# Nine transposes in a row over two PSUM banks with one copy per row half, and some loads in another order

## The chip, the core and the metric

The kernel runs on one core of a Trainium2 chip. The metric is the device time of one execution in microseconds (us), the median of several runs. The kernel before was run three times: 373.53, 374.88 and 376.76 us, so its median is 374.88 us.

Names of the engines: PE is TensorE (matmuls, and transposes as a matmul against an identity), DVE is VectorE, ACT is ScalarE, POOL is GpSimd, SP is the engine that only issues DMAs here. POOL issues DMAs too, and each costs it time. PSUM has 8 banks; PE writes its results there and DVE or ACT copy them out.

## What is computed

Causal attention with a running bias, then a gated feed-forward block over its output, all in one kernel:

```python
scores = q @ k.T / sqrt(64)                    # 8 batches x 8 heads, 576 positions, 64 wide
cum    = cumsum(max(s, 0))
scores = where(causal, -1e9, scores + min(-(cum_i - cum_j), 0))
x      = softmax(scores) @ v                   # -> 4608 tokens x 512
g      = x @ w_gate                            # 512 x 1536
out    = (g * sigmoid(g) * (x @ w_val)) @ w_out    # 1536 x 512
```

Inputs and output are float32; the kernel works in bfloat16 with float32 sums.

## The kernel before, in words

**Units of work.** The 64 heads are taken four at a time: 16 half-batches of four heads. The token rows of the feed-forward block come in 9 tiles of 512 tokens. For one tile 12 gate products and 12 value products of 4 matmuls each are made (lines 643 to 689), then the product with the output weights (line 700, or line 749 with a seven-product scheme in later tiles). The attention of batch b+1 runs between the matmuls of tile b: `ffn_items` yields after each small piece of tile work, and `pump` lets a matching amount of attention work out. All engines run their instructions in the order in which the Python code issues them, so this order is written by hand.

**k and q of a half-batch.** `load_one` brings a [128, 2, 9, 64] float32 tile of k or q; a cast makes it bfloat16 (`cast_one`, `cast_half`). Partition x holds 9 neighbouring positions j, so a half-batch needs 9 transposes of [128, 128] for k and 9 for q, one per j. Rows 0 to 63 of a transposed block belong to one pair of heads, rows 64 to 127 to the other. The blocks lie in PSUM in two groups, j = 0..4 in one bank and j = 5..8 in another (`JG`, line 45). Each group is copied out twice, once for each row half: `pe_out` (line 319) copies a [64, 640] or a [64, 512] block into `KQ`, re-ordering (j, x) into (x, j). So k alone needs four copies, two of 640 and two of 512 elements per partition. From half-batch 5 on, k and q go through DRAM and a DMA transpose instead (`scratch`, `transposes`, `split`).

**PSUM banks.** `take` (line 125) hands out the bank that was given back longest ago, `give` marks it free; this is done while the program is built. At run time an instruction that writes a bank waits for the last reader of that bank.

**The opening (lines 949 to 1033).** Half-batch 0 is prepared by row halves (`row_half`, `row_out`), in the fixed banks `EARLY` = 0, 1 for k and 2, 3 for q. Half-batch 1 is prepared by `half_batch`, which takes four banks; its second row halves are copied after `scores(3)` (lines 996 to 998). POOL casts, issues the loads of v, k, q and of the weights; SP issues others. For half-batch 2 `prep_one` (line 540) is called with i = 0 (k, first group), 1 and 3 (q, both groups) at lines 1026 to 1032, and with i = 2 (k, second group) at item 2 of the first feed-forward tile. `prep_one` copies the first row half at once and puts the copy of the second half on the list `seconds`: that of k is popped at line 1027, those of q one per feed-forward item. k goes to ACT, q to DVE. In between stand the first three gate products, begun by `begin` with the contraction parts that are there (lines 1021 to 1030).

**Hooks.** `at_item(n, ...)` runs a step when tile 0 has done n items (an item is a gate or a value product, 1.0 each, while there are 24 of them). Before: the casts of half-batch 3 at items 9 and 10 and the two halves of the output weights, `w_load("o", 0)` and `w_load("o", 1)`, at items 11 and 13. The casts of batch 1's v (`cast_v`, line 173) are issued on POOL in that same stretch. `load_qk(5)` was issued on SP at line 1016.

Of the kernel before, what the change touches and what calls it, by code (L numbers as in the profile page):

```python
# [13 lines left out]
BF16 = mybir.dt.bfloat16  # L14
# [5 lines left out]
def kernel(  # L20
# [11 lines left out]
    nc = tc.nc  # L32
    PSUM = bass.MemoryType.PSUM

    B, H, S, D = q.shape
# [7 lines left out]
    NR = HB // 2  # L43
    J = 9
    JG = ((0, 5), (5, 9))
# [18 lines left out]
    def pt_col(tj, bi):  # L64
# [26 lines left out]
    KQ = [  # L91
        [const.tile([128, 2, NR * S + 64], BF16, name=f"kq{e}{i}") for e in range(2)]
        for i in range(2)
    ]
    VT = [const.tile([128, NCH, H, D + 1], BF16, name=f"vt{i}") for i in range(2)]
    ident = const.tile([128, 128], BF16)
# [17 lines left out]
    with tc.manual_schedule():  # L114
        loaded = {}
        SRC = {"q": (q, 0), "k": (k, 1)}

        psb = ctx.enter_context(tc.tile_pool(name="psb", bufs=1, space=PSUM))
        banks = psb.tile([128, 8, 512], FP32, name="banks")
        bank = {i: banks[:, i, :] for i in range(8)}  # L120
        released = {i: i - 8 for i in bank}
        clock = [0]
        OPEN = 1 << 40

        def take():
            b = min(bank, key=lambda x: released[x])
            assert released[b] < OPEN
            released[b] = OPEN
            return b

        def give(b):
            clock[0] += 1
            released[b] = clock[0]

        def view(b, w):
            return bank[b][:, 0:w]

        def view16(b, w):
            return bank[b][:, 0 : w // 2].bitcast(BF16)

        def load_one(hb, name, rs=(0, NR), eng=nc.sync):
            b, g = divmod(hb, 2)
            if rs[0] == 0:
                loaded[name, hb] = raw.tile([128, NR, J, D], FP32, tag="raw" + name, name="raw" + name)
            eng.dma_start(
                loaded[name, hb][:, rs[0] : rs[1], :, :].rearrange("x r j d -> x r (j d)"),
                SRC[name][0][b, g * HB + 2 * rs[0] : g * HB + 2 * rs[1], :, :].rearrange(
                    "(r e) (p j) d -> (e p) r (j d)", e=2, j=J
                ),
            )  # L150

        def load_qk(hb):
            load_one(hb, "k")
            load_one(hb, "q")
# [12 lines left out]
        def cast_v(b, c, eng):  # L167
            n = 128 if c < 4 else TAIL
            dst, src_t = VT[b % 2][0:n, c, :, 0:D], loaded["v", b][0:n, c, :, :]
            if eng is nc.scalar:  # L170
                nc.scalar.copy(dst, src_t)
            else:
                eng.tensor_copy(dst, src_t)  # L173
# [79 lines left out]
        def cast_one(hb, name, eng):  # L253
            cts[name, hb] = cp.tile([128, J, NR, D], BF16, tag="c" + name, bufs=2, name="c" + name)
            dst = cts[name, hb].rearrange("x j r d -> x r j d")
            src_t = loaded[name, hb]
            if eng is nc.scalar:
                nc.scalar.copy(dst, src_t)
            else:
                eng.tensor_copy(dst, src_t)  # L260
# [32 lines left out]
        tps = {}  # L293

        def pe_transpose(hb, name, g):
            j0, j1 = JG[g]
            bs = take()
            ps = view16(bs, (j1 - j0) * 128).rearrange("p (j x) -> p j x", x=128)
            ct = cts[name, hb]
            for j in range(j0, j1):  # L300
                nc.tensor.transpose(  # L301
                    ps[:, j - j0, :], ct[:, j].rearrange("x r d -> x (r d)"), ident
                )
            tps[name, g] = [ps, bs, 2]

        def pe_transpose_half(hb, name, g, r):
            j0, j1 = JG[g]
            if r == 0:
                bs = EARLY[name][g]
                ps = view16(bs, (j1 - j0) * 128).rearrange("p (j x) -> p j x", x=128)  # L310
                tps[name, g] = [ps, bs, 2]
            ps = tps[name, g][0]
            ct = cts[name, hb]
            for j in range(j0, j1):
                nc.tensor.transpose(
                    ps[64 * r : 64 * r + 64, j - j0, :], ct[:, j, r, :], ident
                )

        def pe_out(hb, name, g, r, eng):
            j0, j1 = JG[g]  # L320
            kq = SRC[name][1]
            dst = KQ[hb % 2][r][64 * r : 64 * r + 64, kq, 0 : NR * S].rearrange(
                "a (x j) -> a x j", j=J
            )[:, :, j0:j1]
            tp = tps[name, g]
            srcp = tp[0][64 * r : 64 * r + 64].rearrange("a j x -> a x j")
            if eng is nc.scalar:
                nc.scalar.copy(dst, srcp)
            else:
                eng.tensor_copy(dst, srcp)  # L330
            tp[2] -= 1
            if tp[2] == 0:
                give(tp[1])

        def w_load(kind, j, h=None):
            dst = {"g": WG, "v": WV, "o": WO}[kind][j]
            if kind == "o":
                src_ap = moe_w_out[j * WKO * 128 : (j + 1) * WKO * 128, :].rearrange(
                    "(c p) n -> p c n", p=128
                )  # L340
            else:
                w = moe_w_gate if kind == "g" else moe_w_val
                lo, hi = (0, WCH) if h is None else (h * WCH // 2, (h + 1) * WCH // 2)
                src_ap = w[:, j * WCH + lo : j * WCH + hi].rearrange("(c p) n -> p c n", p=128)
                dst = dst[:, :, lo:hi]
            nc.gpsimd.dma_start(dst, src_ap)
# [191 lines left out]
        seconds = []  # L538

        def prep_one(hb, i, eng=None):  # L540
            g, nm = divmod(i, 2)
            nm = ("k", "q")[nm]
            pe_transpose(hb, nm, g)
            if eng is None:
                eng = nc.scalar if nm == "k" else nc.vector
            pe_out(hb, nm, g, 0, eng)
            seconds.append(lambda: pe_out(hb, nm, g, 1, eng))

        PREP_AT = {
            2: {(1, 3): 0, (2, 1): 2, (2, 3): 1, (3, 1): 3},  # L550
# [339 lines left out]
            else:  # L890
                yield from down_seven(tt, hps, sus)

        EARLY = {"k": (0, 1), "q": (2, 3)}
        PICK = (6, 4)
        for i in bank:
            released[i] = OPEN
# [1 line left out]
        def keep_warm(n, b):  # L898
            for _ in range(n):
                nc.tensor.matmul(view(b, 128), ident, ident, start=True, stop=True)  # L900

        def row_half(nm, r):
            for g in range(2):
                pe_transpose_half(0, nm, g, r)

        def row_out(nm, r, *engs):
            for g in range(2):
                pe_out(0, nm, g, r, engs[g])

        def pick(side):  # L910
            b = PICK[side]
# [20 lines left out]
            give(b)  # L932
            give(b + 1)

        def half_batch(nm):
            for g in range(2):
                pe_transpose(1, nm, g)
                pe_out(1, nm, g, 0, nc.vector)

        def scores(h):  # L940
            for ci in range(4):
                score_piece(h, ci)
# [8 lines left out]
        cast_half(0, "q", 0, nc.scalar)  # L951
        aug(0, SP4, range(1, HB))
        aug(1, SP4)
        row_half("k", 0)
        row_out("k", 0, nc.scalar, nc.scalar)
        cast_half(0, "k", 1, nc.gpsimd)
        cast_half(0, "q", 1, nc.gpsimd)
        load_v(0, range(5), nc.gpsimd)
        row_half("q", 0)
        pick(1)  # L960
        pick(0)
        pe_out(0, "q", 0, 0, nc.scalar)
        pe_out(0, "q", 1, 0, nc.vector)
        picked_row(1)
        picked_row(0)
        row_half("k", 1)
        score_piece(0, 0)
        score_piece(0, 1)
        row_half("q", 1)
        row_out("k", 1, nc.vector, nc.vector)  # L970
        cast_one(1, "k", nc.vector)
        row_out("q", 1, nc.vector, nc.vector)
        score_piece(0, 2)
        score_piece(0, 3)
        cast_one(1, "q", nc.gpsimd)
# [6 lines left out]
        load_one(2, "q", eng=nc.gpsimd)  # L982
        w_load("v", 0, 0)
        w_load("v", 0, 1)
        for nm in ("g", "v"):
            w_load(nm, 1, 0)
        load_one(3, "k", eng=nc.gpsimd)
        scores(1)
        half_batch("k")
        score_piece(2, 0)  # L990
        score_piece(2, 1)
        half_batch("q")
        score_piece(2, 2)
        score_piece(2, 3)
        scores(3)
        for nm in ("k", "q"):
            for g in range(2):
                pe_out(1, nm, g, 1, nc.vector)
        cast_v(0, 4, nc.vector)
        aug(2, SP4)  # L1000
        cast_one(2, "k", nc.gpsimd)
        cast_one(2, "q", nc.gpsimd)
        load_one(3, "q", eng=nc.gpsimd)
        for nm in ("g", "v"):
            w_load(nm, 1, 1)
        init_vt(1)
# [6 lines left out]
        aug(3, SP4)  # L1013
        load_v(1, range(5))
        load_qk(4)
        load_qk(5)
        x_pe(0, nc.vector)
        values(4, 5)
        x_pe(1, nc.scalar)
# [3 lines left out]
        begin("g", 1, range(2))  # L1023
        begin("g", 2, range(2))
        x_pe(3, nc.vector)
        prep_one(2, 0)
        while seconds:
            seconds.pop(0)()
        for ft in range(3):
            begin("g", ft, range(2, 3))  # L1030
        for i in (1, 3):
            prep_one(2, i)
        first_sbuf.close()
        PTP[0] = ctx.enter_context(tc.tile_pool(name="later", bufs=1))
        PTP["bufs"] = 5
# [15 lines left out]
        def at_item(n, f, *args):  # L1051
            hook[n].append(lambda: f(*args))

        at_item(2, prep_one, 2, 2)
        at_item(9, cast_one, 3, "k", nc.gpsimd)
        at_item(10, cast_one, 3, "q", nc.gpsimd)
        at_item(11, w_load, "o", 0)
        at_item(13, w_load, "o", 1)
        for tt in range(NTT):
            lo = H * (tt + 1) + LAGS[tt]  # L1060
            hi = min(H * (tt + 2) + LAGS[tt + 1], BH + 2)
# [4 lines left out]
            n = 0  # L1066
# [54 lines left out]
```

## Time and profile before

| what | before |
|---|---|
| median of 3 runs | 374.88 us (373.53 to 376.76) |
| the profiled execution's own time | 373.92 us |
| its span, first to last instruction | 372.0 us |
| granted TensorE clock, mean | 0.998 |
| busy: PE, DVE, ACT, POOL | 363.2, 291.1, 239.9, 212.4 us |
| PE idle between 0 and 20 us / 20 and 30 / 30 and 40 / 40 and 60 | 3.57 / 0.00 / 0.78 / 0.15 us |
| mean busy share of the DMA engines from 20 to 60 us, by tens | 1.17, 1.20, 1.23, 1.11 |

Times in a profile count from the start of the span. "L330" is line 330 of the kernel before. In a view of the chain, each row is a start, a length and the work that the next row waited for or followed; it is followed back from the end of the window. In a table of groups, a row gives line, engine and operation, the shapes, the count, the busy time in us, the mean length of one in ns, and the idle time of the engine ahead of it. In a table of stretches each engine has its busy time and, in brackets, its count, then come the granted clock, the DMA share and GB/s. PE's rows are pipelined: a 128-column transpose is shown with 219 ns, while five in a row start 55 ns apart.

### The profile page before, as it was taken

To read this page: it belongs to the slowest core of one execution; us is meant where nothing else is said; L and a number is where in the kernel's file an instruction comes from. 1 tells how busy PE (TensorE), PEld (TensorE's weight loads), DVE (VectorE), ACT (ScalarE), POOL (GpSimd) and SP (SyncE) were. 2 spreads that over 40 slices of the span, in tenths; PEclk is the share of its full clock that TensorE was granted. 3 is DMA by queue.
4 is the path that set the end of the run, shared out by engine and by line. 5 is a ranking of instruction groups with operands and counts; after the bars stand their busy time and mean duration, and the time that the engine had idled before them with its cause. 6 is when DMAs were issued, how large, how long until landed. Compare 5 with 4: busy or idle time off the path is not lost.

```text
span 372.0 us, 8786 instructions
## 1 busy us (share of the span) xinstructions
PE 363.2 (98%) x3288; PEld 230.3 (62%) x3288; DVE 291.1 (78%) x585; ACT 239.9 (65%) x470; POOL 212.4 (57%) x325
## 2 busy tenths in 40 slices
PE   7899999999999999999999999999999999999996
PEld 6684556655555557855685558655865585476465
DVE  8978776377985899589967897699868867975984
ACT  8877776778886967688757875786565523323321
POOL 8983556955266547594749464955675516315320
PEclk9999999999999999999999999999999999999999
DMA  7999999799879996996789484994142113002003
GB/s 238 220 254 259 215 272 257 239 299 227 252 172 307 199 268 181 162 285 217 214 179 263 160 185 157 265 210 114 40 121 62 35 30 118 0 3 86 28 0 113
DMA packets 97133, 64.21 MB, mean 173 GB/s; under 512 B 77228, under 2 KB 82724, under 8 KB 97092
## 3 DMA queue, kind: packets, MB, share of 16 engines
q1 hardware_dynamic: 84964, 41.46, 46.9%
q0 software_dynamic: 12128, 22.21, 22.7%
q8 instruction: 25, 0.41, 0.5%
q14 instruction: 16, 0.13, 0.1%
HBM read 37.90 MB, written 19.86 MB: 155 GB/s over the span
## 4 chain that ended last, share of the span: by engine, by line
PE 83%; DVE 10%; DMA 2%; ACT 2%; issue 2%; POOL 1%; DVEq 0%; ACTq 0%
PE banks L643 43%; PE banks L749 17%; PE banks L373 9%; PE banks L410 7%; PE banks L700 5%; DVE kq L330 3%; DMA pk<-ks 2%; DVE pp L666 2%; DVE ht L677 1%; DVE kq L288 1%; ACT th L664 1%; POOL vt L173 1%; ACT pt L383 1%; PE banks L459 1%; PE banks L301 0%
## 5 line engine op out<-in xcount | busy, mean ns | idle before, releaser
L383 ACT ACTIVATE pt<-banks 128x512 bf16<-128x512 f32 (+1 forms) x256 | 120.4, 511 | 29.8 <-PE banks L373 17.1
L643 PE MATMUL banks<-XT,wg 128*128 128x512 bf16 x432 | 111.4, 379 | 0.4 <-DVE pp L666 0.3
L643 PE MATMUL banks<-XT,wv 128*128 128x512 bf16 x432 | 110.9, 379 | 0.1
L664 ACT ACTIVATE th<-banks 128x512 bf16<-128x512 f32 x108 | 64.7, 599 | 56.3 <-PE banks L643 51.4
L666 DVE SCALAR_TENSOR_TENSOR pp<-th,banks 128x512 bf16<-128x512 bf16 x108 | 73.7, 682 | 18.3 <-ACT th L664 18.0
L677 DVE SCALAR_TENSOR_TENSOR ht<-pp,banks 128x512 bf16<-128x512 bf16 x108 | 74.1, 687 | 10.3
L373 PE MATMUL banks<-kq 128*128 128x128 bf16 (+4 forms) x576 | 76.4, 240 | 0.8 <-DVE kq L330 0.3
L686 POOL TENSOR_TENSOR ht<-ht 128x512 bf16<-128x512 bf16 x35 | 40.4, 1154 | 53.3 <-DVE su L684 53.2
L373 PEld LDWEIGHTS <-kq 128*128 128x128 bf16 x576 | 46.1, 98 | 30.7 <-issue 2.4
L643 PEld LDWEIGHTS <-wv 128*128 128x128 bf16 x432 | 38.4, 98 | 36.2 <-issue 0.2
L643 PEld LDWEIGHTS <-wg 128*128 128x128 bf16 x432 | 38.4, 98 | 34.1 <-issue 0.7
L410 PEld LDWEIGHTS <-pt 128*128 128x128 bf16 x960 | 41.8, 98 | 17.7 <-issue 0.7
L388 POOL TENSOR_SCALAR_AFFINE_SELECT pt<-pt 128x512 bf16<-128x512 bf16 x56 | 36.6, 653 | 25.9 <-ACT pt L383 21.7
L410 PE MATMUL banks<-vt,pt 128*128 128x65 bf16 x960 | 46.8, 194 | 0.5 <-DVE ot L427 0.4
L444 POOL DMA_DIRECT2D xs<-ot x24 | 21.7, 904 | 30.4 <-DVE ot L427 28.0
L749 PEld LDWEIGHTS <-ht 128*128 128x128 bf16 x336 | 31.2, 98 | 4.3
L427 DVE TENSOR_TENSOR ot<-banks,rc 128x320 bf16<-128x320 f32 x64 | 31.5, 492 | 2.2
L188 POOL DMA_DIRECT2D kq<-HL x48 | 29.2, 610 | 0.0
L700 PE MATMUL banks<-wo,ht 128*128 128x512 bf16 x96 | 25.8, 379 | 0.0
L749 PEld LDWEIGHTS <-su 128*128 128x128 bf16 x252 | 23.6, 98 | 3.3
L814 POOL TENSOR_TENSOR ysb<-ysb 128x512 f32<-128x512 f32 x12 | 15.2, 1269 | 15.3 <-DVE ysb L808 15.3
L749 PE MATMUL banks<-WS,ht 128*128 128x256 bf16 x168 | 22.9, 273 | 0.0
(101 smaller groups left out, 377.2 us busy)
## 6 DMA issues: line engine op xcount, KB each, us to landing
out_dram<-ysb POOLq DMA_DIRECT2D x32, 256.0 KB, 4.0
rawv<-in_v_dram SPq DMA_DIRECT2D x28, 256.0 KB
rawk<-in_k_dram SPq DMA_DIRECT2D x12, 576.0 KB
rawq<-in_q_dram SPq DMA_DIRECT2D x12, 576.0 KB
xs<-ot POOLq DMA_DIRECT2D x24, 160.0 KB, 3.7
ks<-ck SPq DMA_DIRECT2D x11, 288.0 KB
qs<-cq SPq DMA_DIRECT2D x11, 288.0 KB
rawk<-in_k_dram POOLq DMA_DIRECT2D x3, 576.0 KB, 6.0
```

What stands on the lines that cost most here:

```text
L373: nc.tensor.matmul(sc[:, o : o + w], T[:, 1, e * S + 128 * tj : e * S + 128 * (tj + 1)], T[:, 0, e * S + lo : e * S + hi], start=not maske ...
L383: nc.scalar.activation(pt[:, c0 : c0 + n], sc, AF.Exp, scale=0.125)
L388: nc.gpsimd.affine_select(pt[:, 1088:1600], pt[:, 1088:1600], pattern=[[0, 4], [1, 128]], compare_op=ALU.is_ge, fill=zreg, base=0, channel ...
L410: nc.tensor.matmul(av[:, bi * (D + 1) : (bi + 1) * (D + 1)], pt[:, c0 : c0 + 128], VT[b % 2][:, tj, h, :], start=(tj == 0), stop=(tj == bi),)
L427: nc.vector.tensor_mul(ot[:, :, e * D : (e + 1) * D], av3[:, :, 0:D], rc[:, :, None].to_broadcast([128, NCH, D]),)
L643: nc.tensor.matmul(view(bs, TT), w[:, c, f0 : f0 + 128], xt[:, c, :], start=(c == 0), stop=(c == 3),)
L664: nc.scalar.activation(th, pg, AF.Tanh, scale=0.5)
L666: nc.vector.scalar_tensor_tensor(pp, in0=th, scalar=1.0, in1=pg, op0=ALU.add, op1=ALU.mult)
L677: nc.vector.scalar_tensor_tensor(hp[:, 2 * k2 : 2 * k2 + 2, :].rearrange("p a n -> p (a n)"), in0=pp, scalar=0.5, in1=pv, op0=ALU.mult, op ...
L686: (nc.vector if ft == NFT - 1 else nc.gpsimd).tensor_sub(hp[:, 1:3, :], hp[:, 1:4:2, :], hp[:, 0:3:2, :])
L700: nc.tensor.matmul(view(pys[ts_], DM), hps[ft // 2][:, 2 * (ft % 2) + half, c0 : c0 + 128], WO[j][:, ft % WKO, :], start=(ft == 0), stop=( ...
L749: nc.tensor.matmul(ps, lhs(p), rhs(p), start=(first and p == 0), stop=(last and p == NP - 1), skip_group_check=True,)
```

## The change

Half-batches 0, 1 and 2 are now transposed nine blocks in a row into a pair of neighbouring banks: the nine blocks lie back to back, five at the end of the first bank and four at the start of the second (`SLOT` = 3). One copy of [64, 1152] per row half takes all nine. Only the first copy of q of half-batch 0 is still split between ACT and DVE. Half-batch 1 now uses again the fixed banks 0, 1 and 2, 3, which stay out of `take` until its last copies are issued. Half-batch 2 calls `prep_wide`, which picks a pair of neighbouring banks by `take_pair`. All nine transposes of k of half-batch 2 now stand at the place of the first five, with both its copies behind them.

Loads: on POOL's queue k of half-batch 3 moves ahead of the second part of the gate weights, q of half-batch 3 ahead of the cast of k 2, and one value weight part goes between the two casts. k and q of half-batch 5 leave SP for POOL, at items 21 and 23 of tile 0. The output weights move from items 11 and 13 to items 13 and 19.

Some lines that only delete the old helpers are left out.

```diff
+        EARLY = {"k": 0, "q": 2}
+        SLOT = 8 - JG[0][1]
+        def take_pair(name):
+            b = min(range(7), key=lambda x: max(released[x], released[x + 1]))
+            assert max(released[b], released[b + 1]) < OPEN
+            released[b] = released[b + 1] = OPEN
+            EARLY[name] = b
+        def early(name, j0, j1):
+            c0 = EARLY[name] * 1024 + (SLOT + j0) * 128
+            flat = banks.rearrange("p b n -> p (b n)").bitcast(BF16)
+            return flat[:, c0 : c0 + (j1 - j0) * 128].rearrange("p (j x) -> p j x", x=128)
+        def early_transpose(hb, name, r=None):
+            ct = cts[name, hb]
+            for j in range(J):
+                ps = early(name, j, j + 1)[:, 0, :]
+                if r is None:
+                    nc.tensor.transpose(ps, ct[:, j].rearrange("x r d -> x (r d)"), ident)
+                else:
+                    nc.tensor.transpose(ps[64 * r : 64 * r + 64], ct[:, j, r, :], ident)
+        def early_out(hb, name, r, eng, j0=0, j1=J):
...
+            srcp = early(name, j0, j1)[64 * r : 64 * r + 64].rearrange("a j x -> a x j")
...
+        def early_done(name):
+            give(EARLY[name])
+            give(EARLY[name] + 1)
...
+        def prep_wide(hb, nm, eng):
+            take_pair(nm)
+            early_transpose(hb, nm)
+            early_out(hb, nm, 0, eng)
+            def rest():
+                early_out(hb, nm, 1, eng)
+                early_done(nm)
+            seconds.append(rest)
...
-        row_half("k", 0)
-        row_out("k", 0, nc.scalar, nc.scalar)
+        early_transpose(0, "k", 0)
+        early_out(0, "k", 0, nc.scalar)
...
-        pe_out(0, "q", 0, 0, nc.scalar)
-        pe_out(0, "q", 1, 0, nc.vector)
+        early_out(0, "q", 0, nc.scalar, 0, JG[0][1])
+        early_out(0, "q", 0, nc.vector, JG[0][1], J)
...
-        for nm in ("g", "v"):
-            w_load(nm, 1, 0)
         load_one(3, "k", eng=nc.gpsimd)
+        w_load("g", 1, 0)
+        load_one(3, "q", eng=nc.gpsimd)
         scores(1)
-        half_batch("k")
+        early_transpose(1, "k")
+        early_out(1, "k", 0, nc.vector)
...
         cast_one(2, "k", nc.gpsimd)
+        w_load("v", 1, 0)
         cast_one(2, "q", nc.gpsimd)
-        load_one(3, "q", eng=nc.gpsimd)
...
-        load_qk(5)
...
-        prep_one(2, 0)
+        prep_wide(2, "k", nc.scalar)
         while seconds:
             seconds.pop(0)()
         for ft in range(3):
             begin("g", ft, range(2, 3))
-        for i in (1, 3):
-            prep_one(2, i)
+        prep_wide(2, "q", nc.vector)
...
-        at_item(2, prep_one, 2, 2)
...
-        at_item(11, w_load, "o", 0)
-        at_item(13, w_load, "o", 1)
+        at_item(13, w_load, "o", 0)
+        at_item(19, w_load, "o", 1)
+        at_item(21, load_one, 5, "k", (0, NR), nc.gpsimd)
+        at_item(23, load_one, 5, "q", (0, NR), nc.gpsimd)
```

More of the change, by code (lines that the diff above doesn't have):

```diff
@@ L304, in pe_transpose @@
             tps[name, g] = [ps, bs, 2]
[L306 to L312, printed above, removed]
-            ct = cts[name, hb]
[L314 to L317, printed above, removed]
+        EARLY = {"k": 0, "q": 2}
[10 more added lines that the diff above has]
+        def early_transpose(hb, name, r=None):
+            ct = cts[name, hb]
+            for j in range(J):
[5 more added lines that the diff above has]
+        def early_out(hb, name, r, eng, j0=0, j1=J):
+            dst = KQ[hb % 2][r][64 * r : 64 * r + 64, SRC[name][1], 0 : NR * S].rearrange(
+                "a (x j) -> a x j", j=J
+            )[:, :, j0:j1]
+            srcp = early(name, j0, j1)[64 * r : 64 * r + 64].rearrange("a j x -> a x j")
+            if eng is nc.scalar:
+                nc.scalar.copy(dst, srcp)
+            else:
+                eng.tensor_copy(dst, srcp)
+        def early_done(name):
+            give(EARLY[name])
+            give(EARLY[name] + 1)
         def pe_out(hb, name, g, r, eng):
@@ L891, in ffn_items @@
                 yield from down_seven(tt, hps, sus)
-        EARLY = {"k": (0, 1), "q": (2, 3)}
         PICK = (6, 4)
@@ L900, in keep_warm @@
                 nc.tensor.matmul(view(b, 128), ident, ident, start=True, stop=True)
[L902 to L908, printed above, removed]
         def pick(side):
@@ L933, in picked_row @@
             give(b + 1)
[L935 to L938, printed above, removed]
         def scores(h):
@@ L958 @@
         load_v(0, range(5), nc.gpsimd)
-        row_half("q", 0)
+        early_transpose(0, "q", 0)
         pick(1)
         pick(0)
-        pe_out(0, "q", 0, 0, nc.scalar)
-        pe_out(0, "q", 1, 0, nc.vector)
+        early_out(0, "q", 0, nc.scalar, 0, JG[0][1])
+        early_out(0, "q", 0, nc.vector, JG[0][1], J)
         picked_row(1)
         picked_row(0)
-        row_half("k", 1)
+        early_transpose(0, "k", 1)
         score_piece(0, 0)
         score_piece(0, 1)
-        row_half("q", 1)
-        row_out("k", 1, nc.vector, nc.vector)
+        early_transpose(0, "q", 1)
+        early_out(0, "k", 1, nc.vector)
         cast_one(1, "k", nc.vector)
-        row_out("q", 1, nc.vector, nc.vector)
+        early_out(0, "q", 1, nc.vector)
         score_piece(0, 2)
@@ L984 @@
         w_load("v", 0, 1)
-        for nm in ("g", "v"):
-            w_load(nm, 1, 0)
         load_one(3, "k", eng=nc.gpsimd)
+        w_load("g", 1, 0)
+        load_one(3, "q", eng=nc.gpsimd)
         scores(1)
-        half_batch("k")
+        early_transpose(1, "k")
+        early_out(1, "k", 0, nc.vector)
         score_piece(2, 0)
         score_piece(2, 1)
-        half_batch("q")
+        early_transpose(1, "q")
+        early_out(1, "q", 0, nc.vector)
         score_piece(2, 2)
@@ L995 @@
         scores(3)
-        for nm in ("k", "q"):
-            for g in range(2):
-                pe_out(1, nm, g, 1, nc.vector)
+        early_out(1, "k", 1, nc.vector)
+        early_out(1, "q", 1, nc.vector)
+        early_done("k")
+        early_done("q")
         cast_v(0, 4, nc.vector)
```

## The prediction, made before the changed kernel was run

> **What bounds the kernel now.** I read the table of stretches first, to see where PE is idle at all, then the chain of waits in the places that the change touches, then the groups for the prices.
>
> ```profile
> 30.00:35.00 5.00, 4.22 (x28) 2.17 (x26) 4.67 (x8) 4.31 (x8) 0.63 (x1) 1.00 1.22 261
> 35.00:40.00 5.00, 5.00 (x34) 2.68 (x33) 3.60 (x6) 3.56 (x9) 3.18 (x5) 1.00 1.19 255
> 50.00:55.00 5.00, 4.95 (x55) 2.92 (x54) 4.09 (x9) 3.14 (x7) 3.25 (x6) 1.00 1.13 297
> ```
>
> The first busy time is PE's. From 35 us on PE is full: nothing later can take up a delay that PE has at 35 us, and little can be won there. What PE loses lies before 20 us (3.57 us) and between 30 and 35 us (0.78 us). Why, the chain says:
>
> ```profile
> 27.08 0.28 PE banks L301 x5
> 27.36 0.65 PE banks L643 x3
> 28.01 0.29 PE banks L301 x5
> ...
> 28.32 1.46 DVE kq L330 x2
> 29.78 0.57 DVE pp L666
> ...
> 30.38 0.84 DVE kq L330
> ...
> 31.24 0.69 DVE ht L677
> ...
> 31.96 0.72 DVE kq L330
> ...
> 32.71 0.70 DVE pp L666
> ```
>
> From 28.3 us DVE sets the pace: the four copies of q of half-batch 2 stand among the first products' work, until PE takes over at 34.85 us. A second place:
>
> ```profile
> 50.20 1.13 POOL vt L173 x2
> ...
> 51.37 0.19 PE banks L410
> ```
>
> PE waits here for POOL's cast of the fourth piece of v. Ten short matmuls take 51.40 - 50.88 = 0.52 us where 30 ns each make 0.30: a stall of 0.2 us. The prices:
>
> ```profile
> L330 DVE COPY kq<-banks 64x640 bf16<-64x640 bf16 x14 | 11.5, 821 | 1.5 <-PE banks L301 1.3
> L330 DVE COPY kq<-banks 64x512 bf16<-64x512 bf16 x11 | 7.9, 717 | 0.6 <-PE banks L301 0.6
> L328 ACT COPY kq<-banks 64x512 bf16<-64x512 bf16 x9 | 6.5, 717 | 0.4 <-PE banks L301 0.3
> L328 ACT COPY kq<-banks 64x640 bf16<-64x640 bf16 x6 | 4.5, 749 | 0.8 <-PE banks L301 0.8
> L258 ACT CAST ck<-rawk 128x1152 bf16<-128x1152 f32 x10 | 11.6, 1156 | 0.0
> L346 POOL DMA_DIRECT2D wo<-in_moe_w_out_dram x2 | 1.7, 850 | 0.0
> ```
>
> **Price of a wide copy.** No row has it. On DVE a pair costs 821 + 717 = 1538 ns, the upper end; the line through the two shapes (0.81 ns per element) gives 821 + 512 x 0.81 = 1237 ns, the lower end. The shortest and the longest row of this line, 706 and 830 ns, make it 0.97 per element and 1327 ns. I take 1.37 us, a little above that, since a source that changes bank within a row is new. On ACT the pair is 1466 ns (upper), the line through both shapes 877 ns (lower); ACT's row with 1152 elements is the cast with 1156 ns. I take 1.16 us, by the nearest size.
>
> **The opening, 0 to 19 us.** The split copy of q 0 and DVE's row ahead of the first score (line 929, 8.44 to 9.33 us) stay, so the first score stays at 9.38 us. k and q of half-batch 0, second halves, get shorter by 0.17 us each, and k 1 no longer waits for a bank (two waits of PE on DVE, 0.7 us). But the transposes of q 1 wait for POOL's cast, which ends at 13.81 us as before; PE reaches them at 13.9 us either way. They take 0.67 us, so a wide copy starts at 14.63, where the first group's copy began at about 14.41. Three wide copies: 14.63 + 3 x 1.37 = 18.74 us, against 18.79 now. Only four banks remain for the scores until then; ACT's exponentials follow each other (6.45 us for 16) and set that pace. Gain: 0.0, from -0.4 (1.24 us a copy) to +0.5 (1.54).
>
> **Half-batch 2: a new wait.** The two programs' instruction orders, with the waits written in them, show what the diff does not. `take_pair` gives k banks 3 and 4. Both copies of k are issued at once, so banks 3 and 4 are marked free, 3 earlier; for q the pair with the oldest marks is then 2 and 3. The sixth transpose of q is the first to write bank 3, and it carries a wait for ACT's second copy of k. PE works in order, so all behind it waits too.
> - k's nine transposes: 26.92 + 8 x 0.055 + 0.22 = 27.58 us; ACT's first copy starts at 27.62 and the second ends at 27.62 + 2 x 1.16 = 29.94.
> - PE has done three products and five transposes of q by 28.3 us and idles until 29.98, 1.6 us. With four more transposes the first product goes on at 30.20, now 28.35. Four transposes of k that stood at 29.43 (0.22 us) are already done: PE's lag is 1.63 us.
> - DVE starts its copy of q when all nine are done, 29.98 + 0.165 + 0.22 + 0.04 = 30.40, now 28.32. From there to the end of the third pp (34.79) DVE needs 6.47 us, 1.46 + 0.84 + 0.72 = 3.02 of it for four copies. Two wide ones take 2.74, so it ends at 30.40 + 6.19 = 36.59: 1.80 us later.
> - PE's next value product waits for that pp (34.85 now). The lag is the larger one: **+1.80 us**. ACT's tanh is no bound, as its product is later than the copies.
> Bounds: the short copies give 1.80 - 2 x 0.28 - 2 x 0.13 = 0.98, the long ones 1.80 + 2 x 0.31 + 2 x 0.17 = 2.76.
>
> The wait is by bank. [...] By address the ninth transpose would wait instead, since it lies on the columns of k's first block; three transposes (3 x 0.055 us) would come before the stall, and the sum would be 2.5 instead of 2.65.
>
> The trace shows the clock at 1.00 through every stall so far, the longest 0.5 us after the start. [...]
>
> **The output weights ahead of the casts of v.** At item 19 the issue of the second half (0.85 us of POOL) stands between the third and the fourth cast of v. POOL comes to them behind ACT (it waited 2.62 us for ACT ahead of 48.20), so they move with PE, and the fourth cast, for which PE already waits, ends 0.85 us later against PE. Nothing is behind that could take it up: PE has 0.05 us idle from 50 to 55. **+0.85 us**; lower end 0, if POOL came earlier, upper 0.86.
>
> **The other loads.** k and q of half-batch 3 come sooner. The moved weight parts landed 12.2 and 14.3 us after issue, by 35.6 us, and are first used at about 40.1 and 41.7; behind two more loads, 1.5 to 2 us each, there is still room. The first half of the output weights landed 10.5 us after issue, by 50.6, and is needed at 56.0: one affine select later changes nothing. The issues of k and q 5 (0.7 us each) stand in POOL time in which it waited for the data of half-batch 4 (1.66 and 1.48 us), which now have less beside them. 0, upper end in the rival.
>
> **Sum.** 1.80 + 0.85 + 0.0 = 2.65 us. The profiled execution (span 372.0, its own time 373.92) would become 376.6; it stands 0.96 under the median, and against the median I forecast 374.88 + 2.65 = **377.5 us**.
>
> **Rivals.**
> 1. The late loads decide; this one is slower by more than 1%. The second half of the output weights is issued at about 50.75 + 1.80 = 52.55 and needed at 65.69 + 2.65 = 68.3; it may take 15.8 us. Before it took 17.5, beside k and q 5, which now follow it. q 5 is issued near 59 and cast at 66.1 + 2.65 = 68.8, 9.8 us; loads of this kind on POOL's queue took 5.3 to 15.2, median 6.4. For it: the DMA share is over 1 until 60 us. Against: 0.90 after, and less in flight. With 17.5 and 12.4 us they are 1.7 and 2.6 late: 379.2 to 380.1.
> 2. The copies become quick, with whole rows written in one piece. For it: the copy of line 466 from one bank, 576 adjacent elements, took 457 ns, 0.5 per element beyond the fixed part. Against: the source still jumps at every element. With 0.76 on DVE and the lower end of 0.88 on ACT, DVE begins at 30.40 - 0.56 = 29.84 and ends at 29.84 + 3.45 + 1.52 = 34.81, no lag; the opening gains up to 0.55, v costs 0.85: 375.2, no slower.
> 3. The stall does not cost what it says, because later small waits of PE (0.25 near 43 us, 0.2 at 51, 0.26 from 80 to 90, 0.4 from 130 to 140) shrink when DVE and POOL have caught up: at most 1.1 back, 376.4.
>
> **How the numbers follow.** Forecast 0.60, rival 1 0.20, rival 2 0.10, rival 3 0.10. About 1% is what a measurement of this kernel can tell from no change; that is 371.1 to 378.6. The forecast's own bounds: 374.88 + 0.98 + 0 - 0.4 = 375.5 to 374.88 + 2.76 + 0.86 + 0.5 = 379.0. With rival 2 and most of rival 1 the range is 375.0 to 380.0. Slower by over 1%: 0.15 of rival 1 and 0.10 of the forecast's upper part, 0.25. Faster by over 1% needs 3.8 us, more than all of PE's idle time in reach: 0.03. Within 1%: 0.72.
>
> **What would show it.** Right: PE idle about 1.6 us near 28.3 to 30.0 with ACT's copy as the releaser, DVE's copy of q at 30.4, the product that is now at 34.85 at 36.6; a stall near 53.5 behind POOL's v; rows of about 1.37 and 1.16 us. Wrong: wide copies outside 1.24 to 1.54 or 0.88 to 1.47, PE lagging less at 36 than at 30, a wait on DMA for line 700, or the opening's end moved by over 0.5 us.

## The result, and the profile after

| | before | after |
|---|---|---|
| median (22 runs each) | 374.65 us | 376.46 us |
| fastest of them | 373.29 us | 375.80 us |
| the profiled execution's own time / span | 373.92 / 372.0 us | 377.01 / 375.2 us |
| wide copy on DVE / on ACT | 1538 / 1466 ns (two copies) | 1355 / 1112 ns |

The ratio after to before is 1.0045 (95% interval 1.0026 to 1.0063): 1.7 us slower, between 1.0 and 2.4 (the medians lie 1.81 apart). The forecast of 377.5 us was 1.0 too high; its range, 375.0 to 380.0, held the time. A run more than 1.5% above the fastest of its kernel is counted as slow and stays out of the ratios: in this study three of the twelve runs of loads_wo_old and one of before in each of two series.

Line numbers of after: `early_transpose` is L325 (half rows L327), its copies are L335 (ACT) and L337 (DVE), the gate and value products L678, pp and ht L701 and L712, `cast_v` L173, `w_load` L370, scores L397, values L434. The chain of waits of after, 26 to 37 us (start, length, work):

```profile
27.02 0.52 PE banks L325 x9
...
27.56 1.11 ACT kq L335
...
28.68 1.12 ACT kq L335
...
29.84 0.38 PE banks L325 x4
30.23 3.24 PE banks L678 x15
33.47 0.24 PE banks L397 x4
33.70 0.68 DVE ht L712
...
35.78 0.61 DVE pp L701
...
36.43 0.59 PE banks L678 x2
```

Nine transposes of k, both of ACT's wide copies, then the last four transposes of q: PE has made five of q's nine and sits still until ACT has read the bank that q's sixth block goes into. PE's rows for the five and the four (start, length, engine, work, count, and in brackets the idle time ahead of it and what ended it) and DVE's for its copy of q:

```profile
28.00 0.44 PE L325 MATMUL banks<-ident,cq 128*128 128x128 bf16 x5
29.84 0.38 PE L325 MATMUL banks<-ident,cq 128*128 128x128 bf16 x4 [1.40 <-ACT kq L335]
```

```profile
30.33 1.35 DVE L337 COPY kq<-banks 64x1152 bf16<-64x1152 bf16 x1 [2.82 <-PE banks L325]
```

DVE's copies of q started at 28.32 before and start at 30.33 now; two wide copies instead of four narrow ones do not make that up. The value product that began at 34.85 us begins at 36.43. From 30.23 to 33.70 us the chain goes along PE's own products, but DVE's second wide copy (32.31, 1.36 long) ends only 0.03 us sooner, at 33.67. What sets the lag is DVE: PE is 1.50 us late behind the stall, catches up to 0.98 by 34.4 us, as it does not lose again what it lost there before, and then stands still twice more for DVE:

```profile
35.83 0.38 PE L397 MATMUL banks<-kq 128*128 128x128 bf16 x4 [0.34 <-DVE ht L712]
36.43 1.02 PE L678 MATMUL banks<-XT,wv 128*128 128x512 bf16 x4 [0.21 <-DVE pp L701]
```

Behind these waits it is 1.58 us late.

The second place, in the chain of after from 50 to 55 us:

```profile
52.34 0.78 POOL wo L370
53.12 0.63 POOL vt L173
...
53.80 0.19 PE banks L434
```

POOL's issue of the second half of the output weights lies on the path, between two casts of v. PE's row for it:

```profile
53.80 0.19 PE L434 MATMUL banks<-vt,pt 128*128 128x65 bf16 x1 [0.89 <-POOL vt L173]
```

The prices, from after's groups with the shapes kept apart:

```profile
L337 DVE COPY kq<-banks 64x1152 bf16<-64x1152 bf16 x8 | 10.8, 1355 | 3.3 <-PE banks L325 3.1
L335 ACT COPY kq<-banks 64x1152 bf16<-64x1152 bf16 x3 | 3.3, 1112 | 1.0 <-PE banks L325 1.0
```

**A lag, followed through the trace.** Both programs have 3288 weight loads on PE, in the same order but for some twenty near 28 us, where the change moves transposes. The start of the n-th in after, less its start in before, each counted from the first one, is PE's lag. It is -0.1 us at 14 us, -0.07 at 24.5, 1.58 at 33.5 and up to 48, 2.42 from 52 to 125, 1.86 from 135 to 240, and 3.06 from 255 to the end. (This clock starts 1.4 us after the span.) So the change itself is done at 52 us with 2.42. The two later steps do not belong to the change, but to late loads in one or the other execution. In the execution before, DVE waited 0.76 us for a late DMA transpose of k (its copy of line 288 starts at 125.62 us); after's execution had such a wait of 1.74 us, with the copy at 246.20. The chain of after behind it:

```profile
249.61 0.59 issue
250.20 0.68 DVE kq L288
...
251.14 0.50 DVE ot L451
...
251.68 0.46 PE banks L434 x10
```

DVE's second copy of k (line 288) starts 4.0 us behind the first, when DVE is through with the work between them; the copy of the attention result stands behind it, and PE waits 0.43 us for that. In before the same four steps stand at 129.33 to 131.44 us, with 0.40 us for PE. Take the step of the lag out of each, 373.92 - 0.56 = 373.36 and 377.01 - 1.20 = 375.81: each is within 0.1 us of the fastest time of its kernel. Read this way, an execution is a fixed time plus such late loads (in these traces in the opening, at 50 to 60 us and near 95, 117, 126 and 246), which gives a second yardstick beside the median. The fastest times of before in five series of 17 to 35 runs were 373.29, 373.36, 373.37, 373.34 and 373.37; medians of the same series lay between 374.18 and 375.05.

### The profile page after: what moved, and what is told of

Its sections match the earlier page's. It is cut to its first block, busy times and chain, and to the rows that moved or that the text cites. A ratio compares the mean times of both kernels' runs of the same rounds, so it can differ in the third digit from the quotient of the medians.

```text
span 375.2 us, 8727 instructions
## 1 busy us (share of the span) xinstructions
PE 362.1 (97%) x3248; PEld 231.0 (62%) x3288; DVE 290.3 (77%) x577; ACT 239.6 (64%) x467; POOL 213.5 (57%) x327
## 4 chain that ended last, share of the span: by engine, by line
PE 85%; DVE 5%; POOL 4%; ACT 2%; issue 2%; DVEq 0%; POOLq 0%; ACTq 0%
PE banks L678 45%; PE banks L784 17%; PE banks L397 10%; PE banks L434 7%; PE banks L735 5%; DVE pp L701 1%; DVE ht L712 1%; POOL rawv L162 1%; DVE kq L337 1%; DVE kq L288 1%; POOL vt L173 1%; ACT kq L335 1%; ACT pt L407 1%; PE banks L483 1%; ACT th L699 0%
## 5 line engine op out<-in xcount | busy, mean ns | idle before, releaser
L407 ACT ACTIVATE pt<-banks 128x512 bf16<-128x512 f32 (+1 forms) x256 | 120.7, 510 | 31.2 <-PE banks L397 17.5
L678 PE MATMUL banks<-XT,wg 128*128 128x512 bf16 x418 | 110.3, 379 | 1.2 <-DVE ht L712 0.3
L678 PE MATMUL banks<-XT,wv 128*128 128x512 bf16 x412 | 109.3, 379 | 1.2 <-DVE pp L701 0.2
L701 DVE SCALAR_TENSOR_TENSOR pp<-th,banks 128x512 bf16<-128x512 bf16 x108 | 73.5, 681 | 17.9 <-ACT th L699 17.4
L712 DVE SCALAR_TENSOR_TENSOR ht<-pp,banks 128x512 bf16<-128x512 bf16 x108 | 74.0, 686 | 11.1 <-PE banks L678 0.9
L397 PE MATMUL banks<-kq 128*128 128x128 bf16 (+4 forms) x576 | 76.5, 240 | 1.4 <-DVE kq L337 0.6
L397 PEld LDWEIGHTS <-kq 128*128 128x128 bf16 x576 | 46.3, 98 | 31.0 <-issue 2.4
L678 PEld LDWEIGHTS <-wv 128*128 128x128 bf16 x432 | 38.4, 98 | 37.3 <-issue 1.3
L678 PEld LDWEIGHTS <-wg 128*128 128x128 bf16 x432 | 38.4, 98 | 34.5 <-issue 0.9
L434 PEld LDWEIGHTS <-pt 128*128 128x128 bf16 x960 | 41.8, 98 | 17.6 <-issue 0.7
L434 PE MATMUL banks<-vt,pt 128*128 128x65 bf16 x960 | 46.7, 194 | 1.4 <-POOL vt L173 0.9
L735 PE MATMUL banks<-wo,ht 128*128 128x512 bf16 x90 | 24.8, 379 | 0.3
L417 POOL TENSOR_SCALAR_AFFINE_SELECT pt<-pt 128x64 bf16<-128x64 bf16 x56 | 14.7, 262 | 17.2 <-ACT pt L407 17.0
```

What stands on the lines that cost most here:

```text
L397: nc.tensor.matmul(sc[:, o : o + w], T[:, 1, e * S + 128 * tj : e * S + 128 * (tj + 1)], T[:, 0, e * S + lo : e * S + hi], start=not maske ...
L407: nc.scalar.activation(pt[:, c0 : c0 + n], sc, AF.Exp, scale=0.125)
L434: nc.tensor.matmul(av[:, bi * (D + 1) : (bi + 1) * (D + 1)], pt[:, c0 : c0 + 128], VT[b % 2][:, tj, h, :], start=(tj == 0), stop=(tj == bi),)
L678: nc.tensor.matmul(view(bs, TT), w[:, c, f0 : f0 + 128], xt[:, c, :], start=(c == 0), stop=(c == 3),)
L701: nc.vector.scalar_tensor_tensor(pp, in0=th, scalar=1.0, in1=pg, op0=ALU.add, op1=ALU.mult)
L712: nc.vector.scalar_tensor_tensor(hp[:, 2 * k2 : 2 * k2 + 2, :].rearrange("p a n -> p (a n)"), in0=pp, scalar=0.5, in1=pv, op0=ALU.mult, op ...
```

## The experiments

The theory: two waits make the loss, one bank that k and q of half-batch 2 share (1.58 us) and one DMA issue between casts (0.84 us). Rivals: the wide copies are at fault whatever their banks; the loads come late; a lag of PE is paid back later.

All were measured in five rounds beside the kernel before. Lags are read as above, with what single late loads added taken out where a note says so; "fastest" is the fastest time less 373.36.

| run | lag at 33.5 | at 60 | fastest | median | ratio to before (95%) |
|---|---|---|---|---|---|
| after | 1.58 | 2.42 | +2.4 | 376.46 | 1.0045 (1.0026 to 1.0063) |
| apart | 0.45 | 1.30 | +1.3 | 375.31 | 1.0023 (0.9993 to 1.0054) |
| wo_behind | 1.60 | 1.60 | +1.6 | 376.10 | 1.0038 (1.0012 to 1.0065) |
| apart_wo | 0.46 | 0.46 | +1.1 | 375.16 | 1.0032 (1.0008 to 1.0056) |
| transposes_only | 1.65 (a) | 1.65 | +1.6 | 375.44 | 1.0031 (1.0006 to 1.0056) |
| loads_only | 0.0 (a) | 0.84 | +1.2 | 375.46 | 1.0034 (1.0005 to 1.0063) |
| opening_wide | 0.0 (a) | 1.4 (b) | +0.4 | 374.97 | 1.0029 (0.9999 to 1.0059) |
| delayed | 2.36 (a) | 2.36 | +2.4 | 375.95 | 1.0056 (1.0031 to 1.0081) |
| best | 0.25 | 0.26 | +0.1 | 374.52 | 1.0009 (0.9979 to 1.0038) |
| loads_wo_old | 0.44 | 4.99 (b) | +0.2 | 376.32 (c) | 1.0025 (0.9981 to 1.0069) |
| loads_fixed | 0.08 | 0.09 | +0.1 | 374.54 | 1.0008 (0.9978 to 1.0038) |
| k1_early | 2.97 | 3.96 | +2.9 | 376.61 | 1.0038 (1.0005 to 1.0071) |
| best_early | 3.19 | 3.18 | +2.7 | 377.08 | 1.0061 (1.0030 to 1.0092) |

(a) The lag that this execution already had at 24.5 us, from late loads in the opening, is taken off: 1.29, 1.52, 0.69 and 2.09 us. (b) Late data, told below. (c) Median of nine runs.

### Pairs of banks that share none (apart)

```diff
         def take_pair(name):
-            b = min(range(7), key=lambda x: max(released[x], released[x + 1]))
+            b = {"k": 4, "q": 2}[name]
```

> The changed kernel, with k and q of half-batch 2 in pairs of banks that share none (k in 4 and 5, q in 2 and 3). If the shared bank makes the stall: no idle of TensorE before q's sixth transpose, VectorE's copy of q starts at about 28.9 us instead of 30.33; the first tanh still waits for ScalarE's second copy of k, so the third pp ends at about 35.3: the lag against the kernel before at 36 us falls from 1.58 to 0.5, and the time by 1.1 us against the changed kernel. If instead the wide copies by themselves make VectorE late: lag at 36 us stays at 1.3 or more, and the time moves by 0.3 at most.

PE now makes the nine transposes of q without a gap, and DVE's copy starts at 28.79:

```profile
28.02 0.67 PE L325 MATMUL banks<-ident,cq 128*128 128x128 bf16 x9
```

Behind that the chain is the one that was worked out: ACT's two copies, the first tanh, DVE, and the third pp ends at 34.65 + 0.61 = 35.26 us:

```profile
28.70 1.11 ACT kq L335
...
29.83 0.61 ACT th L699
...
34.65 0.61 DVE pp L701
```

The lag falls by 1.13 us, and so do the fastest time (375.80 to 374.68) and the median (by 1.15). The shared bank made that part; the other 0.45 is, by this chain, ACT's second copy of k ahead of the tanh.

### The output weights behind the casts of v (wo_behind), and both repairs (apart_wo)

```diff
-        at_item(19, w_load, "o", 1)
+        at_item(21, w_load, "o", 1)
```

> The changed kernel, with the second half of the output weights issued behind the casts of v (item 21) instead of between them. If GpSimd's issue makes the stall near 53.8 us: the step of 0.85 in TensorE's lag at 52 to 54 us is gone, and the time falls by 0.8 us against the changed kernel. If the casts are late for another reason (ScalarE, the data of v): lag and time stay within 0.2. The weights land 1 to 2 us later, by 62 us, and are needed at 67, so they cost nothing by either.

PE waits for nothing from 48 to 56 us, and POOL's rows show three casts in a row with the issue behind them:

```profile
51.75 1.72 POOL L173 CAST vt<-rawv 128x512 bf16<-128x512 f32 x3
53.42 0.84 POOL L370 DMA_DIRECT2D wo<-in_moe_w_out_dram  x1
```

The lag stays at 1.60, and the fastest time falls by 0.82. The median falls by only 0.36: seven of the twelve runs lie 1.1 us or more above the fastest. In the profiled one a late load (of x, for the product at 120 us) added 1.1 us.

> The changed kernel with both repairs: pairs of banks apart, second half of the output weights behind the casts of v. By the sum of the two: lag 0.45 at 36 us and still 0.45 at 60 us; 1.9 us faster than the changed kernel, 0.4 slower than before. Rival (the weights' place does not matter, as the median of its own run hinted): 1.1 faster than the changed kernel.

The lag is as expected, 0.46 at 36 and 60 us. The times are not: the fastest is 374.49, where 373.8 was expected. In its profiled execution 2.28 us of 374.58 lie outside the span of 372.3, where the other profiled executions have 1.7 to 2.0; what that is, the trace does not show. Another 0.30 us of lag comes at 94 us, where DVE waits 1.5 us for a DMA transpose of k.

Such later steps may be a price of the repair itself. In the profiles of all five versions with the weights at item 21 (wo_behind, apart_wo, and best, loads_fixed and best_early below) PE's lag grows by 0.24 to 1.1 us between 77 and 120 us; four of them have that wait for k near 94 us (1.4 to 1.5 us, against 1.0 in before), wo_behind the late x. Of the other versions only delayed has such a growth (0.19). Why, the traces do not show, and with one profile each it may be chance.

### Each half of the change alone (transposes_only, loads_only)

transposes_only is after with the loads where they were; loads_only is the kernel before with the new order of the loads, the output weights at items 13 and 19 among it.

> All the transposes and copies of the changed kernel, with the loads in the order before. By the forecast's sum: lag 1.6 us at 36 us, no step at 52 to 54 us, 1.6 us slower than the kernel before. Rival (the loads carry the loss): within 0.3 of the kernel before.

> The kernel before, with the loads in the order after. By the forecast's sum: lag 0 at 36 us, 0.85 at 54 us behind GpSimd's fourth cast of v, 0.85 us slower than before. Rival (the transposes carry the loss, the issue is covered): within 0.2 of before. Third way (the earlier k and q 3 take waits away): 0.3 or more faster at 50 us.

In both the step stands where it was expected: transposes_only has PE's wait of 1.4 us for ACT and no step at 52 us; loads_only has no step at 28 us and PE's wait of 0.90 us for POOL's cast of v at 53.7. The first row is of transposes_only (who waited for whom, us in total, times, the longest), the second of loads_only:

```profile
PE banks L325 <- ACT kq L335: 1.4, 1, 1.4
```

```profile
53.73 0.19 PE L410 MATMUL banks<-vt,pt 128*128 128x65 bf16 x1 [0.90 <-POOL vt L173]
```

The fastest times, +1.6 and +1.2, stand beside lags of 1.65 and 0.84; that loads_only is 0.3 above its lag fits with late loads in each of its twelve runs, which is not shown.

### The opening alone (opening_wide)

After's opening, with half-batch 2 and the loads as before.

> The changed kernel's opening (half-batches 0 and 1 with wide copies), with half-batch 2 and the loads as before. By the forecast: lag 0.0 when the values begin (18.9 us), no step at 28 or 52 us, so the time of before within 0.4 us. Rival (the wide copies gain or cost in the opening by themselves): 0.4 or more to one side, and a lag of that size at 19 us.

This execution had late loads. DVE waited 1.3 us for k 1 (lag 0.7 at 14 us), and POOL for v and for k 4 at 50 to 60 us (another 1.4). So its lag does not measure the copies. That they cost nothing is better read in after, apart, wo_behind and apart_wo, where the lag at 24.5 us is -0.07 to -0.04. The fastest time is +0.4, the edge between what was expected and the rival, so it decides nothing. The spans speak against the rival: the shortest of this version is 371.3 us, in a run of 374.51 us of which 3.2 lie outside the span, and the shortest of before is 371.4.

### Does a lag at 28 us last? (delayed)

```diff
             bs = take()
+            if (hb, name, g) == (2, "k", 0):
+                for _ in range(11):
+                    nc.tensor.matmul(view(bs, 512), ident, lower[:, 0:512], start=True, stop=True)
```

> The kernel before, with 11 matmuls of 512 columns (2.4 us of TensorE by 216 ns each) put ahead of k's transposes of half-batch 2; they are overwritten and change no result. Tells whether a lag at that place costs its size to the end. If it does: lag 2.4 at 36 us and 2.4 us slower. If later small waits pay a part back (rival 3 of the forecast): lag falls near 43 or 130 us, and the time is 1.3 to 1.9 us slower.

The lag rises from 2.09 (late loads in the opening) by 2.36 to 4.45 and stays there to 110 us. The fastest time is 375.75, and five of twelve runs lie within 0.02 of it: 2.38 above before, just 11 x 0.216 (three matmuls of 512 columns take 0.65 us at 27.36 us in the chain of before). So nothing is paid back in this profile or in the fastest time. The step of -0.56 between 125 and 135 us, which after shows too, is in all runs of this study: it is the late load of the profiled execution before. But the median is only 1.7 above that of before (374.25), within the 1.3 to 1.9 that the rival gave, since more executions lie near the fastest time. So executions with late loads may pay a part back, which no trace here shows.

### Can the transposes win? (best)

```diff
-        while seconds:
-            seconds.pop(0)()
+        prep_wide(2, "q", nc.vector)
         for ft in range(3):
             begin("g", ft, range(2, 3))
-        prep_wide(2, "q", nc.vector)
```

with both repairs. k's second copy now follows the first tanh. (Two things move at once, so the share of each is not told apart.)

> Both repairs, and q's transposes of half-batch 2 ahead of the three gate products, with ScalarE's second copy of k behind the first tanh. VectorE's copy of q starts at about 28.2, the first tanh ends at 29.35, and the third pp ends at about 34.35, 0.45 before that of the kernel before: lag -0.45 to 0 at 36 us, and a time 0 to 0.5 under before. Rival (TensorE must wait for the first pp ahead of the second value product, about 30.3): lag 0.5 to 0.8, and no faster than before.

The lag is 0.25, of which 0.24 was there at 24.5 us: half-batch 2 costs nothing now. It also gains nothing. The wait that the rival named is there, but the lag is below the rival's 0.5 to 0.8: PE waits 0.33 us for the first pp ahead of the second value product and 0.21 for the third. No difference of the time from that of before is shown.

### The loads (loads_wo_old, loads_fixed, k1_early, best_early)

loads_wo_old is loads_only with the output weights back at items 11 and 13; loads_fixed is loads_only with the second half at item 21.

> The kernel before with the new order of the loads, but the output weights where they were (items 11 and 13). If only the place of the weights costs: lag 0 at 54 us, fastest time 373.4 (that of before) where the full new order has 374.54. If the other loads bring something in the slower executions: median up to 0.5 under before. Rival (the earlier k and q 3 and later k and q 5 cost by themselves): lag or fastest time 0.5 or more above.

The fastest time is 0.2 above that of before, so the other loads need not cost anything. But the median is 1.7 us higher (376.32 against 374.67), and the interval of the ratio reaches from 0.998 to 1.007: whether this order brings late data more often stays open. In the profiled execution the data of v came late: PE waited 2.99 us at 52 to 55 us. The stretches around it show what that did to the clock (the number behind POOL's count; the next is the DMA share):

```profile
53.00:54.00 1.00, 0.00 (x0) 0.00 (x0) 0.00 (x0) 0.00 (x0) 0.00 (x0) 1.00 1.14 294
...
55.00:56.00 1.00, 1.00 (x8) 0.49 (x6) 0.00 (x0) 0.00 (x0) 0.63 (x2) 0.73 0.59 169
56.00:57.00 1.00, 1.00 (x22) 1.00 (x20) 0.91 (x3) 0.00 (x0) 0.99 (x3) 0.50 0.37 112
...
58.00:59.00 1.00, 1.00 (x4) 0.34 (x3) 0.01 (x1) 0.23 (x1) 0.91 (x2) 0.57 1.18 315
```

The DMA engines are busy all through the wait (share 1.03 to 1.14), so v was not alone on them; which load held it up, the trace does not settle. Then the clock is at half for 3.4 us, and the lag goes on from 3.38 to 4.99.

> The kernel before with the new order of the loads and the second half of the output weights behind the casts of v (item 21): no wide copies. If GpSimd's issue was the whole cost of the loads and the later weights keep the data of v and of k and q 4 in time: lag 0 at 60 us, no wait of GpSimd on a load between 46 and 66 us, fastest time 373.4 and median 373.7 to 374.2, 0.2 to 0.8 under before. Rival (the later data were chance, and nothing is gained): median within 0.2 of before. Another: fastest time 0.5 or more above before, so that the earlier loads of k and q 3 cost by themselves.

No lag at 60 us, fastest time as before, and no wait of POOL on a load from 46 to 66 us, where it waited 1.66 and 1.48 us for k and q 4 before; ahead of that it waited 1.57 us for k 2. The median is 0.5 under that of its own series (375.05), but the interval of the ratio spans 1. So a gain is not shown.

k1_early is before with GpSimd's issues of k and q 1 ahead of the memsets, best_early the same in best.

> The kernel before, with GpSimd's issues of k and q of half-batch 1 ahead of its five memsets of the k and q tiles, 2.2 us earlier (at 2.6 us instead of 4.85). In four of the ten profiles so far VectorE or TensorE waited 0.6 to 1.9 us in the opening for these loads or the rows behind them, in the others not. If these waits lift the median above the fastest time (374.2 against 373.4): no wait on k 1 in its profile, the fastest time as before within 0.3, the median 0.3 to 0.8 lower. Rival (the transfers only displace those of half-batch 0): the first scores come later, fastest and median 0.3 or more higher.

> The version with both repairs and q first, with the earlier issues of k and q 1 as well. If the opening's waits lift the median: fastest time 373.5, as without, median 0.3 to 0.8 under before, so a version that beats both. Rival: no difference to the version without (374.5).

k1_early's rival holds, and best_early loses as much, which neither of its two readings allowed for. The transfers of k and q 1, issued at 2.51 and 3.41 us, displace those of half-batch 0. POOL's rows of k1_early:

```profile
8.83 0.66 POOL L271 CAST ck<-rawk 128x576 bf16<-128x576 f32 x1 [2.15 <-DMA rawk<-in_k_dram]
10.65 0.67 POOL L271 CAST cq<-rawq 128x576 bf16<-128x576 f32 x1 [1.16 <-DMA rawq<-in_q_dram]
```

POOL waits 2.15 and 1.16 us for the second rows of half-batch 0, which it cast at 6.54 and 7.41 without waiting before. Every run of both versions is 2.7 us or more over 373.36. My reading of the opening's late loads was no guide to a remedy. No version of this study is shown to beat the kernel before.

## Why the prediction was right, and where its sum was off

- **The new wait at half-batch 2**: right in place, releaser and mechanism (the sixth transpose of q waits for ACT's second copy of k, by bank and not by address: five blocks are done ahead of the wait). The term was 1.80 and measured 1.58. ACT's copy took 1.11 instead of 1.16 us and began 0.06 earlier, so that its second copy ended at 29.80 instead of 29.94 (0.14); DVE's two copies took 1.355 instead of 1.37 each (0.03); the rest are small steps between. PE's own lag behind the stall was 1.50 where 1.63 was forecast, and DVE's path is the longer one, as forecast.
- **The output weights between the casts of v**: 0.85 forecast, 0.84 measured (1.58 to 2.42), and gone in wo_behind.
- **The opening**: 0.0 forecast, -0.07 measured at 24.5 us.
- **Rival 1, late loads**: fell. The second half of the output weights landed 8.3 us after its issue, by 60.6, and was needed at 68; q 5 landed at 65.9 and was cast at 68.5. The 17.5 us that it had taken before did not come again in after (in delayed, k1_early, loads_wo_old and opening_wide, with the weights at item 13, it was 16.1 to 18.3).
- **Rival 2, quick copies**: fell with 1355 and 1112 ns. The fixed part that it takes off line 466's 457 ns is an estimate of mine: 457 - 576 x 0.5 leaves 169 ns, beside DVE's rows of one and of five elements in before with 150 to 156 and 190 ns (lines 219 to 221 and 426).
- **Rival 3, paid back later**: fell in the profiles. The small waits that it named did not shrink, and delayed shows a lag of 2.36 that lasts, to the end and in the fastest time. The wait at 130 us that it counted on was a late load of one execution. In the medians it is open: see the total.
- **The total**: 2.65 forecast; 2.42 of lag; 2.51 between the fastest times; 1.81 between the medians. Of the miss of 1.07 us (377.53 - 376.46), 0.23 is the median of three runs, 374.88, against 374.65 in 22; 0.14 is the sum against the difference of the fastest times; the largest part, 0.70, is that the runs of before scatter more: their median lies 1.36 above the fastest, that of after 0.66. The step that failed is the one that set a sum from one profile on top of a median as if the scatter were the same. Why a later PE scatters less stays open. delayed has the same trait (0.20), with the loads as before, so it isn't the new order of the loads alone; wo_behind (1.12), with the loads and a lag of 1.60, hasn't. Against before, the median rose less than the fastest time in after (by 0.70), delayed (0.68), transposes_only (0.29), apart_wo (0.21) and apart (0.19), but more in wo_behind (0.30): a lag that is partly paid back where loads come late would fit the five, and is not shown.

The sum has no term for the clock: it takes 1.00 through a stall of 1.6 us, where the trace of before shows no stall longer than 0.5 us after the start. For this stall that came out right (1.40 us, with 1.00 from 26 to 36 us in after). In k1_early the clock fell after stalls of 1.52 and 0.37 us: see the last section.

## What to carry to other kernels

A wider copy is only as good as what it must wait for: here 0.2 to 0.35 us saved per copy pair cost a wait of 1.4, as two tiles that used to have four banks in turn were given neighbouring pairs with one bank in common. When a planner gives out buffers, read the waits of the built program, not the allocation rule; and when a DMA issue moves on an engine that also casts, look at who awaits that engine's next result: here PE did, and the issue cost its whole time (0.84 us). Follow the lag of one engine's n-th instruction between two traces: steps that stay are the change, and steps that differ between executions are not.

## What the runs showed of the hardware that was not expected

- The granted clock fell to 0.50 in three runs long before the program's end, which the forecast had not counted on, and each time for 3.4 us (worked out from the clock in stretches of 1 us): after 2.99 us of idle PE in loads_wo_old; in k1_early after 1.52 us and, 1.5 us later, 0.37; in delayed, in the opening, after 1.78 and 0.20. It stayed at 1.00 after 2.17 us in loads_only and 1.40 in after. In the 3.4 us ahead of the three falls PE's rows were busy for about 0.21, 0.47 and 0.42 of the time; in any 3.4 us around after's stall for 0.59 or more, but in the 3.4 us that end with loads_only's stall for only 0.36. So neither the length of the stall nor this share alone puts the falls apart from the rest, and what decides is not shown. The rows of k1_early in steps of 1 us:

```profile
8.00:9.00 1.00, 0.03 (x2) 0.00 (x0) 0.97 (x2) 0.78 (x1) 0.17 (x1) 1.00 1.04 419
...
11.00:12.00 1.00, 0.63 (x8) 0.63 (x8) 0.97 (x2) 0.91 (x2) 1.00 (x2) 0.76 0.08 24
12.00:13.00 1.00, 1.00 (x10) 0.70 (x8) 0.97 (x2) 0.00 (x0) 1.00 (x2) 0.50 0.25 41
```

  PE is busy again from 9.55 us on, but for the 0.37 us, and the clock falls 2 us later. No version was built to try the clock by itself.
- One copy that reads across two banks costs less than two: DVE's 1152 elements took 1355 ns in after where 640 and 512 took 821 and 717 in before, ACT's 1112 against 749 and 717. On DVE that is 118 ns more than the line through the two smaller shapes gives (1.04 ns per element between the two larger shapes, 0.81 between the smaller). Whether the change of bank has a part in it, no run here tells.
- In k1_early two loads of 576 KB were issued 2.3 us earlier (at 2.51 and 3.41 us instead of 4.85 and 5.75), and the casts of two 288 KB loads (k and q of half-batch 0, second rows, issued at 2.53 and 3.00 us in before) began 2.3 and 3.2 us later (8.83 and 10.65 instead of 6.54 and 7.41).
